# Order of the three products of a split feed-forward: high weights twice in a row, low weights last

## The chip, the core and the metric

The kernel runs on one core of a Trainium2 chip. The metric is the device time of one execution in microseconds (us); where several executions are timed, their median counts. TensorE (PE) multiplies; its weight loads are rows of their own (PEld) in the profile. VectorE (DVE), ScalarE (ACT) and GpSimd (POOL) do the elementwise work, and the queue of SyncE (SP) issues most DMAs.

## The reference

```python
def _attn_ref(q, k, v, w_phi):            # 8 x 8 heads, 576 tokens, head_dim 64
    def phi(x):
        proj = np.einsum('bhsd,df->bhsf', x, w_phi)                # 128 features
        proj = proj - np.max(np.abs(proj), axis=-1, keepdims=True)
        return np.concatenate([np.exp(proj), np.exp(-proj)], axis=-1)
    q_p, k_p = (phi(q), phi(k))
    kv = np.einsum('bhsf,bhsd->bhfd', k_p, v)
    z = np.sum(k_p, axis=2)
    num = np.einsum('bhsf,bhfd->bhsd', q_p, kv)
    den = np.einsum('bhsf,bhf->bhs', q_p, z)[..., None] + 1e-06
    return (num / den).astype(np.float32)

def _moe_ref(x, w_in, w_out, alpha):      # x: 4608 x 512, w_in: 512 x 2048, w_out: 2048 x 512
    h = x @ w_in
    g = np.maximum(h, 0.0) + alpha * np.minimum(h, 0.0)
    return (g @ w_out).astype(np.float32)
```

The attention's output, with its heads laid side by side, is the `x` of the feed-forward. All arrays are float32, and the weights of the feed-forward arrive as 64-bit numbers, which the kernel decodes.

## The kernel before

**Attention.** 32 pairs of heads are worked off one after the other (`attention_units`). Each pair loads its keys and queries, projects them (L302), subtracts the largest magnitude, takes exponentials, sums keys times values (L343) and keys alone (L360, with a tile of ones as the stationary operand), turns the sums and the queries (L375, L386, L389), multiplies (L408, L426), divides, and stores 64 x 2 rows of `x` to HBM.

**Feed-forward.** A number is split into a high part of type fp32r (a rounding copy, `rnd`, L123) and a low part, the rest (a subtraction, `low`, L127). A product of two split matrices is made of three matmuls that add up in one PSUM bank: high by high, and the two mixed ones. Weights of one hidden block `ff` (128 of the 2048 hidden units) are four tiles: `wt[0]` and `wt[1]` are the high and low part of `w_in`, `wt[2]` and `wt[3]` those of `w_out`, and all four are 128 x 512 slots of one SBUF tile. Tokens come in 9 chunks of 512. `gemm1` makes one hidden block of a chunk: four steps over the 512 input features, each of three matmuls with 128 x 128 weights and 512 columns of activations (L498 to L500). ACT then takes two rectifiers out of PSUM (L230, L231), DVE joins them (L235), ACT casts the high part `gh` (L123), and DVE subtracts it to get the low part `gl` (L127). `gemm2` adds one hidden block into one of four output blocks `m`, with three matmuls (L504 to L506).

**Two passes.** The first pass holds the weights of 5 of the 16 hidden blocks in SBUF. Its `gemm1` and `gemm2` triples (names `h`, `o`) for a chunk are strewn between the matmuls of later head pairs, in an order written out by hand: every unit has a due time, and the units are issued by it with the order of PE, SP, DVE and ACT pinned (L733). `x` is cast by ACT and its low part is made by POOL (`split`, `split_low`). The partial sums go to HBM (`part_d`). The second pass, with the other 11 hidden blocks (names `h`, `po`), starts between units of the first (L718 to L723) and has the machine to itself from about 607 us on. There the order within each engine is not pinned: a planner, which simulates the program with costs of its own, sets it, so that one triple's matmuls may stand apart with those of other triples between them. Two hidden blocks lie between a `gemm1` and its `gemm2` (`LAG`), and `gh` and `gl` have three buffers each. At the end of a chunk DVE adds the partial sums to the four banks (L690) and SP stores the result.

**SBUF places in the second pass.** The split `x` of even chunks (`x2hl`) lies in the lower part of each partition, that of odd chunks (`x2h`, `x2l`) in the upper part; `gh`, `gl` and the weights of 8 hidden blocks lie low, those of the last 3 high.

Of the kernel before, what the change touches and what calls it, by code (L numbers as in the profile page):

```python
# [24 lines left out]
NK = DM // P  # L25
# [83 lines left out]
def fused_kernel(ctx: ExitStack, tc: tile.TileContext, kq, v, w_phi, w_in, w_out, alpha, out):  # L109
    nc = tc.nc  # L110
    act, dve, pool, pe = nc.scalar, nc.vector, nc.gpsimd, nc.tensor
# [110 lines left out]
    last = [None]  # L222
# [270 lines left out]
    def gemm1(ps, wt, xs, steps=range(NK)):  # L493
        for n in steps:
            j = NK - 1 - n
            ws = slice(j * P, (j + 1) * P)
            xh, xl = xs[j]
            pe.matmul(ps, lhsT=wt[0][:, ws], rhs=xh, start=n == 0, stop=False)  # L498
            pe.matmul(ps, lhsT=wt[1][:, ws], rhs=xh, start=False, stop=False)  # L499
            pe.matmul(ps, lhsT=wt[0][:, ws], rhs=xl, start=False, stop=n == NK - 1)  # L500

    def gemm2(ps, wt, m, gh, gl, first, last):
        ws = slice(m * P, (m + 1) * P)
        pe.matmul(ps, lhsT=wt[2][:, ws], rhs=gh, start=first, stop=False)  # L504
        pe.matmul(ps, lhsT=wt[3][:, ws], rhs=gh, start=False, stop=False)  # L505
        pe.matmul(ps, lhsT=wt[2][:, ws], rhs=gl, start=False, stop=last)  # L506

    def ffn1_units(c, fg=FG):
        cs = slice(c * C2, (c + 1) * C2)
# [24 lines left out]
        def up(ff, n):  # L534
            if n == 0:
                cur["ps"] = psf.tile([P, C2], F32, tag="f", name=f"h1_{c}_{ff}")
            gemm1(cur["ps"], W[ff], gs[0], (n,))
            if n == NK - 1:
                ga[ff] = act_g(cur["ps"], ff, C2, g1p, g1p, GB, f"1_{c}_{ff}", dve, 3)
                ga[ff][0]()  # L540

        def down(m, ff):
            if ff == 0:
                cur["po", m] = psf.tile([P, C2], F32, tag="f", name=f"o1_{c}_{m}")
            gemm2(cur["po", m], W[ff], m, *gs[ff + 1], ff == 0, ff == NF1 - 1)
# [120 lines left out]
    def up2(c, ff):  # L666
        ps = psf.tile([P, C2], F32, tag="f", name=f"h2_{c}_{ff}")
        gemm1(ps, W[NF1 + ff], xs[c])
        gq[c, ff] = act_g(ps, NF1 + ff, C2, late_pools["x2p"], late_pools["x2r"], G2_BUFS, f"2_{c}_{ff}", dve, 3)
# [6 lines left out]
    def down2(c, ff):  # L676
        cs = slice(c * C2, (c + 1) * C2)
        if ff == 0:
            po[c] = [late_pools["pso"].tile([P, C2], F32, tag=f"o{m}", name=f"po{c}{m}") for m in range(NK)]
        if ff == NF2 - 4:  # L680
            prt[c] = x2b[0].tile([P, NK, C2], F32, tag="pt", name=f"pt{c}")
            ld_ = nc.sync.dma_start(prt[c], part_d[:, :, cs].rearrange("k p s -> p k s"))
            if c > 0:
                tc.keep_in_program_order(ld_)
        gh, gl = gq.pop((c, ff))
        for m in range(NK):
            gemm2(po[c][m], W[NF1 + ff], m, gh, gl, ff == 0, ff == NF2 - 1)
            if ff == NF2 - 1:
                o = prt[c][:, m]
                dve.tensor_tensor(o, po[c][m], o, op=ALU.add)  # L690
                if c == NC2 - 1:
                    nc.sync.dma_start(out[m * P : (m + 1) * P, cs], o)
        if ff == NF2 - 1 and c < NC2 - 1:
            nc.sync.dma_start(out[:, cs].rearrange("(m p) s -> p m s", p=P), prt[c])
# [92 lines left out]
```

## Time and profile before

| | us |
|---|---|
| median of 3 runs (1142.69 to 1146.83) | 1143.23 |
| the profiled execution | 1141.93 |
| its span, first to last instruction | 1139.8 |
| PE busy | 1120.0 (98%) |
| DVE busy | 632.7 (56%) |
| ACT busy | 560.5 (49%) |
| POOL busy | 209.4 (18%) |

The profiled execution lies 2.13 us outside its span, and 1.30 us below the median of the runs. Matmul records overlap, since a matmul's end is modelled; the distance from one start to the next is what a matmul takes on PE. A matmul is two records, a weight load on PEld and the matmul on PE; where the instruction waits for a semaphore, its weight load waits.

### The profile page before, as it was taken

Reading aid. Unit: us, or ns where it says so; the run is one execution under the profiler, and the core shown is the slowest. Engines: PE = TensorE matmul, PEld = TensorE weight load, DVE = VectorE, ACT = ScalarE, POOL = GpSimd, SP = SyncE. Lnnn points to the kernel's source line nnn. Section 1 sums busy time; section 2 is a strip of 40 time slices with the busy share of each in tenths; the row PEclk is TensorE's granted clock in tenths of the full one; section 3 lists DMA queues with packets and bytes.
Section 4 is the critical chain, followed back from the end, with each engine's and each line's share of the span. In section 5 each row is a group of like instructions: output and inputs, shape, how many; then the busy total and the mean of one; then the engine's idle time right before and its main releaser. Section 6 shows DMA issues by size and latency. Waiting matters only on the chain.

```text
span 1139.8 us, 18355 instructions
## 1 busy us (share of the span) xinstructions
PE 1120.0 (98%) x7232; PEld 866.8 (76%) x7232; DVE 632.7 (56%) x978; ACT 560.5 (49%) x1149; POOL 209.4 (18%) x213
## 2 busy tenths in 40 slices
PE   7999999999999999999999999999999999999998
PEld 6766777777777777677778888888888888888886
DVE  7888958798788777835862242424242423333322
ACT  5777655666675765664544332333332323333232
POOL 1345332322324142243540000000000000000000
PEclk9999999999999999999999999999999999999999
DMA  5566264546545364566426030303030302011021
GB/s 190 152 186 213 67 200 154 168 151 209 161 149 190 110 211 152 156 219 207 156 65 221 1 112 1 111 1 111 0 111 1 111 1 87 26 38 74 1 74 37
DMA packets 71605, 130.53 MB, mean 115 GB/s; under 512 B 14432, under 2 KB 22752, under 8 KB 70496
## 3 DMA queue, kind: packets, MB, share of 16 engines
q1 hardware_dynamic: 70080, 120.90, 33.1%
q0 software_dynamic: 1152, 8.39, 2.0%
q8 instruction: 57, 0.93, 0.4%
q14 instruction: 28, 0.23, 0.1%
q10 hardware_dynamic: 288, 0.07, 0.0%
HBM read 92.35 MB, written 36.85 MB: 113 GB/s over the span
## 4 chain that ended last, share of the span: by engine, by line
PE 89%; DVE 5%; DMA 4%; ACT 1%; issue 1%; POOL 0%; SPq 0%; DVEq 0%; ACTq 0%; POOLq 0%
PE h L498 11%; PE h L500 11%; PE h L499 11%; PE po L506 8%; PE po L504 8%; PE po L505 8%; PE kv L343 6%; PE n L408 5%; PE pj L302 5%; PE o L506 3%; PE o L504 3%; PE o L505 3%; PE d L426 3%; PE qt L389 2%; PE kv L360 1%; DVE m L306 1%
## 5 line engine op out<-in xcount | busy, mean ns | idle before, releaser
L235 DVE SCALAR_TENSOR_TENSOR g<-r,aln,g 128x512 f32<-128x512 f32 x144 | 112.5, 781 | 318.5 <-ACT g L231 318.5
L230 ACT ACTIVATE r<-h 128x512 f32<-128x512 f32 x144 | 86.5, 601 | 300.1 <-PE h L500 300.0
L506 PE MATMUL po<-gl,w 128*128 128x512 f32 x396 | 154.6, 392 | 1.5 <-DVE gl L127 1.5
L504 PE MATMUL po<-gh,w 128*128 128x512 f32 x396 | 155.1, 392 | 0.1
L505 PE MATMUL po<-gh,w 128*128 128x512 f32 x396 | 155.0, 391 | 0.0
L127 DVE TENSOR_TENSOR gl<-g,gh 128x512 fp32r<-128x512 f32 x144 | 104.8, 728 | 66.9 <-ACT gh L123 66.5
L123 ACT CAST gh<-g 128x512 fp32r<-128x512 f32 x144 | 90.0, 625 | 84.7 <-DVE g L235 84.6
L506 PEld LDWEIGHTS po<-gl,w 128*128 128x128 f32 x396 | 74.3, 188 | 18.8 <-DVE gl L127 2.4
L504 PEld LDWEIGHTS po<-gh,w 128*128 128x128 f32 x396 | 74.3, 188 | 17.0 <-ACT gh L123 0.5
L231 ACT ACTIVATE g<-h 128x512 f32<-128x512 f32 x144 | 85.9, 596 | 2.6 <-DMA part_d<-os 2.6
L505 PEld LDWEIGHTS po<-gh,w 128*128 128x128 f32 x396 | 74.3, 188 | 16.5
L498 PE MATMUL h<-x2hl,w 128*128 128x512 f32 x220 | 86.0, 391 | 0.0
L500 PE MATMUL h<-x2hl,w 128*128 128x512 f32 x220 | 86.0, 391 | 0.0
L499 PE MATMUL h<-x2hl,w 128*128 128x512 f32 x220 | 85.9, 391 | 0.0
L306 DVE TENSOR_REDUCE m<-pj 128x8 f32<-128x1024 f32 (+1 forms) x66 | 78.2, 1185 | 9.6 <-PE pj L302 9.3
L302 PE MATMUL pj<-w_sb,raw 64*128 64x128 f32 x1024 | 74.5, 286 | 7.5 <-DMA w_sb<-w_phi_dram 4.2
L302 PEld LDWEIGHTS pj<-w_sb,raw 64*128 64x128 f32 x1024 | 65.2, 194 | 21.1 <-issue 14.7
L185 POOL TENSOR_TENSOR aw<-ew,aw 128x256 f32<-128x256 f32 x64 | 56.4, 882 | 128.9 <-DVE ew L180 128.9
L307 DVE TENSOR_TENSOR t<-pj,m 128x1024 f32<-128x1024 f32 (+1 forms) x66 | 78.7, 1192 | 2.3
L504 PE MATMUL o<-gh,w 128*128 128x512 f32 x180 | 76.0, 422 | 2.2 <-ACT os L549 2.0
L498 PE MATMUL h<-xh,w 128*128 128x512 f32 x180 | 75.8, 421 | 0.0
L458 POOL TENSOR_TENSOR s<-s,rr 128x576 f32<-128x576 f32 x32 | 47.5, 1485 | 150.4 <-DMA rr<-rec_d 127.2
(84 smaller groups left out, 2132.3 us busy)
## 6 DMA issues: line engine op xcount, KB each, us to landing
xr<-x_d SPq DMA_DIRECT2D x18, 1024.0 KB
raw<-kq_dram SPq DMA_DIRECT2D x31, 576.0 KB
v<-v_dram SPq DMA_DIRECT2D x32, 320.0 KB
rr<-rec_d SPq DMA_DIRECT2D x64, 144.0 KB
x_d<-s SPq DMA_DIRECT2D x32, 288.0 KB
part_d<-os SPq DMA_DIRECT2D x36, 256.0 KB
pt<-part_d SPq DMA_DIRECT2D x9, 1024.0 KB
raww<-w_in_dram SPq DMA_DIRECT2D x32, 256.0 KB
```

The costliest lines, as they stand in the source:

```text
L123: return act.copy(dst, src)
L127: return eng.tensor_tensor(dst, src, f(hi), op=ALU.subtract)
L230: act.activation(st["r"], ps, AF.Relu, scale=-1.0)
L235: dve.scalar_tensor_tensor(g, st["r"], aln[:, ff : ff + 1], g, op0=ALU.mult, op1=ALU.add)
L302: pe.matmul(dst[h, j], lhsT=c["raw"][hs, ts], rhs=w_sb[hs], start=True, stop=True)
L306: dve.tensor_reduce(m, src, axis=AX.X, op=ALU.max, apply_absolute_value=True)
L498: pe.matmul(ps, lhsT=wt[0][:, ws], rhs=xh, start=n == 0, stop=False)
L499: pe.matmul(ps, lhsT=wt[1][:, ws], rhs=xh, start=False, stop=False)
L500: pe.matmul(ps, lhsT=wt[0][:, ws], rhs=xl, start=False, stop=n == NK - 1)
L504: pe.matmul(ps, lhsT=wt[2][:, ws], rhs=gh, start=first, stop=False)
L505: pe.matmul(ps, lhsT=wt[3][:, ws], rhs=gh, start=False, stop=False)
L506: pe.matmul(ps, lhsT=wt[2][:, ws], rhs=gl, start=False, stop=last)
```

## The change

In both helpers the second and third product change places. What is multiplied and summed is the same, and so are the start and stop flags of the first and last matmul.

```diff
@@ gemm1
             pe.matmul(ps, lhsT=wt[0][:, ws], rhs=xh, start=n == 0, stop=False)
-            pe.matmul(ps, lhsT=wt[1][:, ws], rhs=xh, start=False, stop=False)
-            pe.matmul(ps, lhsT=wt[0][:, ws], rhs=xl, start=False, stop=n == NK - 1)
+            pe.matmul(ps, lhsT=wt[0][:, ws], rhs=xl, start=False, stop=False)
+            pe.matmul(ps, lhsT=wt[1][:, ws], rhs=xh, start=False, stop=n == NK - 1)
@@ gemm2
         pe.matmul(ps, lhsT=wt[2][:, ws], rhs=gh, start=first, stop=False)
-        pe.matmul(ps, lhsT=wt[3][:, ws], rhs=gh, start=False, stop=False)
-        pe.matmul(ps, lhsT=wt[2][:, ws], rhs=gl, start=False, stop=last)
+        pe.matmul(ps, lhsT=wt[2][:, ws], rhs=gl, start=False, stop=False)
+        pe.matmul(ps, lhsT=wt[3][:, ws], rhs=gh, start=False, stop=last)
```

So L499 and L505 of the kernel after multiply the low activations, and L500 and L506 the low weights. In a triple, the first and second matmul now name the same stationary tile.

## Rows read from the trace of the kernel before

**Rows 1.** The page, part 1: engine, busy us, share of the span, instructions
```profile
PE 1120.0 (98%) x7232; PEld 866.8 (76%) x7232; DVE 632.7 (56%) x978; ACT 560.5 (49%) x1149; POOL 209.4 (18%) x213
```

**Rows 2.** Busy time by stretches: us, then each engine's busy us (instructions), PEclk, DMA share, GB/s
```profile
100.00:300.00 200.00, 197.80 (x1674) 144.16 (x1673) 158.68 (x234) 128.68 (x278) 67.12 (x60) 1.00 0.51 160
...
500.00:560.00 60.00, 57.48 (x268) 44.16 (x267) 36.42 (x62) 32.83 (x71) 26.68 (x29) 1.00 0.67 226
...
900.00:1000.00 100.00, 100.00 (x437) 81.83 (x436) 33.43 (x49) 34.65 (x62) 0.00 (x0) 1.00 0.19 64
```

**Rows 3.** Groups by line: names, shapes, count | busy us, mean ns | idle us before, releaser
```profile
L506 PE MATMUL po<-gl,w 128*128 128x512 f32 x396 | 154.6, 392 | 1.5 <-DVE gl L127 1.5
...
L506 PE MATMUL o<-gl,w 128*128 128x512 f32 x180 | 71.7, 398 | 3.5 <-DVE gl L127 3.3
L500 PE MATMUL h<-xl,w 128*128 128x512 f32 x180 | 70.7, 393 | 0.0
...
L505 PEld LDWEIGHTS po<-gh,w 128*128 128x128 f32 x396 | 74.3, 188 | 16.5
...
L360 PEld LDWEIGHTS kv<-z,ones 128*32 128x32 f32 x184 | 3.6, 108 | 3.0 <-issue 0.4
```

**Rows 4.** Waits of PEld: line, releaser, us in total, times, longest us
```profile
PEld o L506 <- DVE gl L127: 7.1, 9, 2.0
...
PEld po L506 <- DVE gl L127: 2.4, 2, 1.8
```

**Rows 5.** Timeline, PEld, 201 to 204 us: start us, us, operation, idle before
```profile
201.78 0.19 PEld L505 LDWEIGHTS o<-gh,w 128*128 128x128 f32 x1
202.01 0.19 PEld L506 LDWEIGHTS o<-gl,w 128*128 128x128 f32 x1
...
202.90 0.19 PEld L505 LDWEIGHTS o<-gh,w 128*128 128x128 f32 x1
203.72 0.19 PEld L506 LDWEIGHTS o<-gl,w 128*128 128x128 f32 x1 [0.62 <-DVE gl L127]
```

**Rows 6.** Timeline, DVE, the same stretch
```profile
201.23 0.68 DVE L127 TENSOR_TENSOR gl<-g,gh 128x512 fp32r<-128x512 f32 x1
...
202.99 0.68 DVE L127 TENSOR_TENSOR gl<-g,gh 128x512 fp32r<-128x512 f32 x1
```

**Rows 7.** Timeline, PEld, two pairs of waits that follow closely
```profile
517.22 0.19 PEld L506 LDWEIGHTS o<-gl,w 128*128 128x128 f32 x1 [0.48 <-DVE gl L127]
...
518.97 0.19 PEld L506 LDWEIGHTS o<-gl,w 128*128 128x128 f32 x1 [1.21 <-DVE gl L127]
...
540.82 0.19 PEld L506 LDWEIGHTS po<-gl,w 128*128 128x128 f32 x1 [1.80 <-DVE gl L127]
...
544.36 0.19 PEld L506 LDWEIGHTS po<-gl,w 128*128 128x128 f32 x1 [0.59 <-DVE gl L127]
```

**Rows 8.** Timeline, DVE and ACT, before the second wait of each pair
```profile
518.24 1.45 DVE L127 TENSOR_TENSOR gl<-g,gh 128x512 fp32r<-128x512 f32 x2
...
542.32 0.60 ACT L231 ACTIVATE g<-h 128x512 f32<-128x512 f32 x1 [2.63 <-DMA part_d<-os]
```

**Rows 9.** Timeline, POOL and PE, a low part of x and its first reader
```profile
548.06 2.76 POOL L127 TENSOR_TENSOR xl<-xr,xh 128x512 fp32r<-128x512 f32 x2
...
551.80 0.39 PE L499 MATMUL h<-xh,w 128*128 128x512 f32 x1
```

**Rows 10.** Timeline, PE, ten matmuls on low x and low weights: first and last
```profile
717.68 0.39 PE L499 MATMUL h<-x2hl,w 128*128 128x512 f32 x1
...
719.72 0.39 PE L499 MATMUL h<-x2hl,w 128*128 128x512 f32 x1
```

**Rows 11.** Timeline, PE, ten matmuls on high x and low weights: first, last
```profile
673.20 0.40 PE L498 MATMUL h<-x2h,w 128*128 128x512 f32 x1
...
675.30 0.39 PE L504 MATMUL po<-gh,w 128*128 128x512 f32 x1
```

## The prediction

> **What bounds the kernel now.** I read the page's first part, then busy time by stretches, then PE's groups by line, then the waits of PE's weight loads, and the timeline around those waits last. The first part gives the bound: PE is busy for 98% of the span, DVE for 56% [rows 1]. The stretches show that it isn't bound in the same way throughout. From 900 to 1000 us, in the second pass, PE has no gap at all at a granted clock of 1.00, the 2.4 GHz level, while DVE and ACT work for a third of the time; around 200 us it is still 99% busy, but DVE is at 79%; between 500 and 560 us PE loses 2.5 of 60 us [rows 2]. So in the second pass only the distance from one matmul to the next counts, and in the first also whether an operand is ready in time. In the second pass 437 records touch those 100 us; two of them only reach in over an edge, so 435 starts lie in it and the mean distance is 100/435 = 229.9 ns.
>
> The reader is to see in the groups that every matmul has its weight load: the page counts 7232 of either [rows 1], and a load takes 188 ns, less than the distance, and lies beside the matmul in front [rows 3]. PE's own idle time names one releaser among the feed-forward's lines that bears on the change: `gl`, ahead of L506, 1.5 us for `po` and 3.3 us for `o` [rows 3]. That is only the visible part. The wait is taken by the weight load, and there it is 7.1 us in 9 times and 2.4 us in 2: eleven waits, 9.5 us [rows 4]. All lie before 545 us or in the rest of the first pass; none is in the second pass proper.
>
> **What the change does, part by part.** *The matmuls.* Per triple, three before and three after, 1152 triples (9 chunks x 16 hidden blocks x 4 steps, once for each helper), no instruction added or gone, the same shapes. PE's stream costs the same if the distance does, taken as 0 here; its two bounds are worked out under the rivals.
>
> *The low activations are needed one matmul sooner.* This is the one cost that the order itself carries. A weight load is issued when the matmul in front of it starts. In a triple today the load for `gl` goes out at the start of the second product; afterwards at the start of the first. Where `gl` is already late, its end doesn't move; behind it there are now two matmuls of the triple left instead of one. So each of the eleven waits grows by one distance, 0.23 us, and pushes everything behind it on PE: the third product, the rest of the triples, and with them ACT, which relieves PSUM. 11 x 0.23 = 2.5 us.
>
> *New waits.* A `gl` that comes ready in the last 0.23 us before its load is late afterwards. Comparing DVE's 144 subtractions with the first load that reads each, I find one: `gl` ends at 201.91 (201.23 + 0.68) [rows 6], its load goes out at 202.01, and in the new order would go out with the load that now starts at 201.78 [rows 5]: a wait of 0.13 us, and up to another 0.1 us because the load isn't hidden any more. I take 0.2 us. The very next one is of the eleven: DVE works until 203.67 [rows 6] and the load starts at 203.72 after 0.62 us [rows 5].
>
> *What comes back.* Two pairs of waits stand so close that the first one's delay runs into the second. At 517.2 and 519.0 us [rows 7] the second wait's DVE work is queued behind DVE work of its own [rows 8]; at 540.8 and 544.4 [rows 7] the second hangs on ACT, which itself waited 2.6 us for a DMA [rows 8]. In both the second wait shrinks by what the first grew: -2 x 0.23 = -0.5 us.
>
> *The other low operand.* `xl` of the first pass is made by POOL far ahead: the tightest of the 36 I find ends at 550.82 (548.06 + 2.76), and its load goes out at 551.80 with the matmul in front [rows 9], 0.98 us later, four distances. The group of its reader shows no idle time [rows 3]. Cost 0. If POOL were a microsecond later there, it would be one wait of the kind above.
>
> *Buffers.* `gh` and `xh` are read until the third product now, so they come free 0.23 us later, `gl` and `xl` sooner. No wait of PE names such a release; the cover is three to five buffers with two hidden blocks between writer and reader. Cost 0; without that cover, 0.23 us per buffer turn. No DMA and no instruction of SP, POOL, ACT or DVE moves in the pinned part.
>
> **Sum.** 2.5 + 0.2 - 0.5 = 2.2 us, between 0 (PE's delay swallowed each time by a later wait on something that PE doesn't feed) and 2.8 (no delay swallowed). On the profiled execution 1141.9 + 2.2 = 1144.1; the median of the runs shown lies 1.3 us above it, so 1143.2 + 2.2 = 1145.4, a change of 0.2%. A difference under 0.5% (5.7 us) is about what a measurement of this kernel can't tell from none, so this forecast is "no change" with a lean to slower.
>
> **Rivals.**
>
> *The second load of the same weights falls away.* Two matmuls in a row now name one stationary tile, so a load could be left out, by the build or in the engine. Price: a matmul without a load can't be shorter than its 512 columns; at one column a cycle of 2.4 GHz, which I assume, that is 213.3 ns, so at most 229.9 - 213.3 = 16.6 ns for each of 1152 second products, 19.1 us; at least 0, since the load of 188 ns is hidden already [rows 3]. At the full price 1145.4 - 19.1 = 1126.3. Against it: all 184 matmuls with the tile of ones as stationary operand, one after another in groups, have 184 loads of their own [rows 3], though at changing places of the array. For it: nothing but the kernel's new order. The Trainium skill ("TensorE: Matmul & The Clock Gate", section "Step-by-step: what each phase is for") says that weights often stay put over many matmuls, and that load and compute are separate so that one can load once and multiply repeatedly. The same page's section "Back-to-back issue gap" gives 518 cycles for an isolated matmul of 512 columns, 215.8 ns; by that, an estimate, the gain would be 16.2 us. By that rule the time falls by over 1%; the trace, with a load for every matmul, does not show it.
>
> *The hand-over gets slower (the case on the other side).* The trace has two distances. Nine distances with `x` in the lower part of SBUF and low weights take 719.72 - 717.68 = 2.04 us, 226.7 ns each [rows 10]; nine with `x` in the upper part and low weights take 2.10 us, 233.3 ns [rows 11]. It seems to depend on which tile streams while which weights are loaded, and the change makes new pairs: high activations beside the load of the same weights again, low ones beside the low weights. Should every pair of the second pass (9 x 11 x 8 x 3 = 2376 matmuls) come out slow, that is 2376 x 3.4 ns = 8.1 us: 1153.5, slower by 0.9%. It decides from about half of them on. Against it: inside either stretch all three kinds of hand-over have the same distance, and the tiles paired anew lie in the same parts of SBUF as before. The mirror image, every pair fast, is 2376 x -3.2 = -7.6 us: 1137.8.
>
> *The planner orders the second pass anew.* Its order is not written down, and a low operand that is due earlier can make it draw triples apart elsewhere. If it then starts each of the 8 later chunks with a wait as long as the longest shown, 2.0 us [rows 4], that is 16 us: 1161. Against it: PE has no gap there, `gl` is made two hidden blocks ahead, and the order has a microsecond and more to give.
>
> *The change doesn't reach the waits*, since all are swallowed: 1143.2. It is inside the forecast's own range.
>
> **Chances and range.** The forecast, waits alone, 0 to 2.8 us: 0.84, own range 1142 to 1148 with the spread of the runs shown, whose highest is 3.6 us over the median. Load left out: 0.04. Slow hand-overs: 0.05; fast ones: 0.03. A worse order: 0.04. Faster by over 0.5% means under 1137.5: load left out, and a little of the fast hand-overs: 0.05. Slower means above 1148.9: slow hand-overs, a worse order at its price, without the part of either that stays small: 0.07. The range of 1141 to 1149 leaves out mainly the outer cases.
>
> **What would show it.** In the changed profile the wait on `gl` should stand at L505 (now the low activations) instead of L506, eleven or twelve times for PEld, each about 0.23 us longer, and the weight loads should still count 7232. L499 and L500 should have no idle time, 900 to 1000 us should hold 436 to 438 matmuls, and the distances in the two shown stretches should be 227 and 233 ns. Fewer loads or over 440 matmuls in those 100 us would make the first rival right; 430 or fewer the second; a gap of PE after 607 us that names `xl`, `x2l` or `gl` the third.

## The result, and the profile after

The kernel after takes 1146.34 us (median of 22 runs, 1143.38 to 1149.01), the kernel before 1143.69 us (22 runs beside them, 1141.42 to 1148.66): a ratio of 1.0019, 95% interval 1.001 to 1.0028, that is 1.1 to 3.2 us slower. Forecast were 2.2 us, called "no change" with a lean to slower.

The first part of the page after, where the counts of matmuls and loads are what they were [rows 1]:

```profile
span 1143.5 us, 18355 instructions
...
PE 1118.3 (98%) x7232; PEld 865.1 (76%) x7232; DVE 636.3 (56%) x978; ACT 560.9 (49%) x1149; POOL 210.6 (18%) x213
```

Groups of the kernel after by line, which answer to [rows 3]. L499 and L505 multiply the low activations now:

```profile
L505 PE MATMUL po<-gl,w 128*128 128x512 f32 x396 | 155.2, 392 | 2.0 <-DVE gl L127 2.0
L506 PE MATMUL po<-gh,w 128*128 128x512 f32 x396 | 154.9, 391 | 0.0
...
L505 PE MATMUL o<-gl,w 128*128 128x512 f32 x180 | 71.6, 398 | 5.5 <-DVE gl L127 5.3
...
L499 PE MATMUL h<-xl,w 128*128 128x512 f32 x180 | 70.5, 392 | 0.0
```

Waits of the weight loads after (line, releaser, us in total, times, longest), beside [rows 4]:

```profile
PEld o L505 <- DVE gl L127: 9.4, 10, 2.2
...
PEld po L505 <- DVE gl L127: 2.7, 2, 2.0
```

The wait on `gl` has gone with its operand from L506 to L505: twelve times and 12.1 us instead of eleven and 9.5. The low part of `x` has still no wait (L499). The second pass shows nothing. Here are its busy time from 900 to 1000 us (columns as in [rows 2]), and the first and tenth of ten matmuls with low and with high `x` [rows 10, 11]:

```profile
900.00:1000.00 100.00, 100.00 (x437) 81.84 (x436) 35.26 (x52) 35.53 (x64) 0.00 (x0) 1.00 0.19 64
```

```profile
720.49 0.39 PE L498 MATMUL h<-x2hl,w 128*128 128x512 f32 x1
...
722.53 0.39 PE L498 MATMUL h<-x2hl,w 128*128 128x512 f32 x1
```

```profile
676.21 0.40 PE L498 MATMUL h<-x2h,w 128*128 128x512 f32 x1
...
678.31 0.40 PE L498 MATMUL h<-x2h,w 128*128 128x512 f32 x1
```

Nine distances are 2.04 and 2.10 us again, 226.7 and 233.3 ns; the count is the same 437.

Two profiles of this kernel can't be subtracted from end to end, since executions differ by microseconds in the first 230 us whatever the kernel. So I read three marks in each profile: A, the start of the same key-value matmul of the attention; B and C, the starts of the first and the last addition of partial sums (L690). First the kernel before (A is the start in the row of the timeline, B and C are the two times in the row of the tile's operations), then the kernel after:

```profile
227.43 1.95 PE L343 MATMUL kv<-xk,v 128*64 128x256 f32 x16
```

```profile
L690 DVE TENSOR_TENSOR pt<-po,pt x36: 681/685/692, 654.0 to 1136.0; 128x512 f32<-128x512 f32 x36
```

```profile
229.24 1.95 PE L343 MATMUL kv<-xk,v 128*64 128x256 f32 x16
```

```profile
L690 DVE TENSOR_TENSOR pt<-po,pt x36: 678/683/692, 657.7 to 1139.7; 128x512 f32<-128x512 f32 x36
```

The same marks of all kernels, us:

| kernel | A | B | C | A to B | B to C |
|---|---|---|---|---|---|
| before | 227.43 | 654.0 | 1136.0 | 426.6 | 482.0 |
| after | 229.24 | 657.7 | 1139.7 | 428.5 | 482.0 |
| e1, gemm1 alone | 230.39 | 656.9 | 1138.9 | 426.5 | 482.0 |
| e2, gemm2 alone | 227.85 | 656.2 | 1138.3 | 428.4 | 482.1 |
| e3, same pairs, low last | 227.78 | 654.7 | 1136.8 | 426.9 | 482.1 |
| e4, low first | 230.63 | 661.4 | 1143.4 | 430.8 | 482.0 |
| e5, held back | 229.40 | 651.1 | 1133.1 | 421.7 | 482.0 |
| e6, places | 229.59 | 655.1 | 1133.8 | 425.5 | 478.7 |
| e7, e5 and e6 | 229.62 | 652.4 | 1131.1 | 422.8 | 478.7 |
| e8, e7 and copy first | 226.28 | 646.2 | 1125.0 | 419.9 | 478.8 |
| e9, copy first | 226.88 | 654.2 | 1136.2 | 427.3 | 482.0 |

The kernel after loses 1.9 us between A and B, where ten of the eleven waits lie, and nothing between B and C, where 2096 of the second pass's 2376 matmuls start. What lies ahead of A, 1.8 us in this pair of profiles, is of the size by which kernels with the very same program up to there differ: e6 reaches A 2.2 us later than the kernel before. A to B isn't free of that either: the five kernels with `gl` third in `gemm2` and no product held back (before, e1, e3, e6, e9) take 425.5 to 427.3 us, and most of their differences arise at one place, near 543 us, where PE hangs on a DMA. So the 1.9 us are also followed from wait to wait, where the prediction is gone through step by step.

### The profile page after: what moved, and what is told of

It reads as the page before. It is cut to its first block, busy times and chain, and to the rows that moved or that the text cites. A ratio compares the mean times of both kernels' runs of the same rounds, so it can differ in the third digit from the quotient of the medians.

```text
span 1143.5 us, 18355 instructions
## 1 busy us (share of the span) xinstructions
PE 1118.3 (98%) x7232; PEld 865.1 (76%) x7232; DVE 636.3 (56%) x978; ACT 560.9 (49%) x1149; POOL 210.6 (18%) x213
## 3 DMA queue, kind: packets, MB, share of 16 engines
q0 software_dynamic: 1152, 8.39, 2.0%
## 4 chain that ended last, share of the span: by engine, by line
PE 88%; DVE 5%; DMA 4%; ACT 1%; issue 1%; POOL 0%; SPq 0%; DVEq 0%; ACTq 0%; POOLq 0%
PE h L498 11%; PE h L499 11%; PE h L500 11%; PE po L505 8%; PE po L506 8%; PE po L504 8%; PE kv L343 6%; PE n L408 5%; PE pj L302 5%; PE o L505 3%; PE o L504 3%; PE o L506 3%; PE d L426 2%; PE qt L389 2%; DVE m L306 1%; PE kv L360 1%
## 5 line engine op out<-in xcount | busy, mean ns | idle before, releaser
L505 PE MATMUL po<-gl,w 128*128 128x512 f32 x396 | 155.2, 392 | 2.0 <-DVE gl L127 2.0
L506 PE MATMUL po<-gh,w 128*128 128x512 f32 x396 | 154.9, 391 | 0.0
L505 PEld LDWEIGHTS po<-gl,w 128*128 128x128 f32 x396 | 74.3, 188 | 19.2 <-DVE gl L127 2.7
L506 PEld LDWEIGHTS po<-gh,w 128*128 128x128 f32 x396 | 74.3, 188 | 16.4
L500 PE MATMUL h<-x2hl,w 128*128 128x512 f32 x220 | 86.0, 391 | 0.0
L499 PE MATMUL h<-x2hl,w 128*128 128x512 f32 x220 | 85.9, 391 | 0.0
L505 PE MATMUL o<-gl,w 128*128 128x512 f32 x180 | 71.6, 398 | 5.5 <-DVE gl L127 5.3
```

The costliest lines, as they stand in the source:

```text
L499: pe.matmul(ps, lhsT=wt[0][:, ws], rhs=xl, start=False, stop=False)
L500: pe.matmul(ps, lhsT=wt[1][:, ws], rhs=xh, start=False, stop=n == NK - 1)
L505: pe.matmul(ps, lhsT=wt[2][:, ws], rhs=gl, start=False, stop=False)
L506: pe.matmul(ps, lhsT=wt[3][:, ws], rhs=gh, start=False, stop=last)
```

## The experiments

The theory is that the cost comes from the eleven waits alone, because `gl` is needed one matmul sooner. The rival is a cost of the hand-over: the same weights loaded twice in a row, with a little lost (or a load saved) at each of 1152 triples.

**e1_up_only.** The new order in `gemm1` only:

```diff
 pe.matmul(ps, lhsT=wt[0][:, ws], rhs=xh, start=n == 0, stop=False)
-pe.matmul(ps, lhsT=wt[1][:, ws], rhs=xh, start=False, stop=False)
-pe.matmul(ps, lhsT=wt[0][:, ws], rhs=xl, start=False, stop=n == NK - 1)
+pe.matmul(ps, lhsT=wt[0][:, ws], rhs=xl, start=False, stop=False)
+pe.matmul(ps, lhsT=wt[1][:, ws], rhs=xh, start=False, stop=n == NK - 1)
```

> The new order in gemm1 alone; gemm2 keeps the old one. Theory of the waits (the whole cost comes from gl being needed one matmul sooner): 0 us against the kernel before, within 1 us either way, since xl has 0.98 us and more in hand; waits on gl stay at L506, eleven, about 9.5 us for the weight loads. Rival of the hand-over (a cost spread evenly over the 1152 triples, since the same weights are loaded twice in a row): half of what the whole change costs, 1.3 us, and the distances of matmuls in the second pass longer than 227 and 233 ns.

Measured: 1144.12 us, ratio 1.0004 (0.9992 to 1.0016). From A to B 426.5 us against 426.6, B to C 482.0 against 482.0. Half of the triples in the new order cost nothing that shows in the profile; the interval of the timing, -0.9 to 1.8 us, would by itself still hold the rival's 1.3 us.

**e2_down_only.** The same exchange in `gemm2` only:

```diff
 pe.matmul(ps, lhsT=wt[2][:, ws], rhs=gh, start=first, stop=False)
-pe.matmul(ps, lhsT=wt[3][:, ws], rhs=gh, start=False, stop=False)
-pe.matmul(ps, lhsT=wt[2][:, ws], rhs=gl, start=False, stop=last)
+pe.matmul(ps, lhsT=wt[2][:, ws], rhs=gl, start=False, stop=False)
+pe.matmul(ps, lhsT=wt[3][:, ws], rhs=gh, start=False, stop=last)
```

> The new order in gemm2 alone; gemm1 keeps the old one. Theory of the waits: the whole cost, 2.2 us (1.5 to 3.2) over the kernel before; the weight loads at L505 wait for gl eleven or twelve times, about 12 us, nothing changes after 607 us. Rival of the hand-over: half of it, 1.3 us, part of it in the second pass.

Measured: 1146.65 us, ratio 1.0025 (1.001 to 1.0039): the whole cost. Between A and B 428.4 us, 1.8 more than before; nothing in the second pass. Its loads wait eleven times, 11.2 us in all:

```profile
PEld o L505 <- DVE gl L127: 8.5, 9, 2.2
...
PEld po L505 <- DVE gl L127: 2.7, 2, 2.0
```

**e3_low_last_pairs.** Low weights first in both helpers, so that the two products with high weights stand together as in the change, but the low activations come third as before:

```diff
-pe.matmul(ps, lhsT=wt[2][:, ws], rhs=gh, start=first, stop=False)
-pe.matmul(ps, lhsT=wt[3][:, ws], rhs=gh, start=False, stop=False)
+pe.matmul(ps, lhsT=wt[3][:, ws], rhs=gh, start=first, stop=False)
+pe.matmul(ps, lhsT=wt[2][:, ws], rhs=gh, start=False, stop=False)
 pe.matmul(ps, lhsT=wt[2][:, ws], rhs=gl, start=False, stop=last)
```

> Both helpers with low weights first, then high weights with high and then low activations: the same weights twice in a row as in the change, but the low activations third as in the kernel before. Theory of the waits: 0 us against the kernel before (within 1 us), eleven waits on gl of about 9.5 us at L506. Rival of the hand-over: the full 2.7 us of the change. Rival of the load that falls away: fewer than 7232 weight loads, up to 19 us faster.

Measured: 1143.21 us, ratio 0.9991 (0.9978 to 1.0005). The first part of its page and its waits:

```profile
PE 1120.4 (98%) x7232; PEld 866.7 (76%) x7232; DVE 633.2 (56%) x978; ACT 560.9 (49%) x1149; POOL 212.4 (19%) x213
```

```profile
PEld o L506 <- DVE gl L127: 7.4, 10, 2.0
...
PEld po L506 <- DVE gl L127: 2.4, 2, 1.8
```

The reader is to see three things: no load falls away with the same weights twice in a row, the waits have their old size (9.8 us), and the time is that of the kernel before: the interval ends 0.6 us above it, and the rival asked for 2.7 us. So the pairing is neither the cost nor a gain; what costs is where the low activations stand. That decides between the two theories. Every matmul brings its own load here, 7232 of either, and the same weights twice in a row 1152 times saved nothing. The Trainium skill ("TensorE: Matmul & The Clock Gate", section "Step-by-step: what each phase is for") says that load and compute are separate so that one can load once and multiply repeatedly; in this program's trace that did not happen.

**e4_low_first.** The dose doubled: in `gemm2` the low activations first of the three, then the two with `gh`.

> gemm2 with the product of the low activations first of the three, then the two of the high ones; gemm1 as before. The dose is doubled: gl is needed two matmuls sooner than in the kernel before. Theory of the waits: each of the eleven waits 0.46 us longer, 5.1 us, plus about 0.4 us for the one gl that just missed, less about 0.9 us where two waits follow closely: 4.5 us (3 to 6), all before 607 us. Rival of the hand-over (the same weights twice in a row, as in the change): no more than the change, 2.7 us or, for gemm2 alone, 1.3 us.

Measured: 1148.53 us, ratio 1.0035 (1.002 to 1.005), slower by 2.3 to 5.7 us. Between A and B 430.8 us, 4.2 more than before where the change itself has 1.9; nothing in the second pass. One distance earlier costs 1.9, two cost 4.2.

**e5_hold_back.** The other way round, from the kernel before. In the first pass `gl`'s product of a triple is kept back by two triples; for the first three blocks of the second pass it comes behind the high products of all four banks:

```diff
+            gemm2_high(cur["po", m], W[ff], m, gs[ff + 1][0], ff == 0)
+            held.append((m, ff))
+            if ff == NF1 - 1:
+                own = [h for h in held if h[0] == m]
+                for h in own:
+                    held.remove(h)
+                    low_part(*h, h is own[-1])
+            elif len(held) > HOLD:
+                low_part(*held.pop(0), False)
...
+        if c == 0 and ff < NB:
+            for m in range(NK):
+                gemm2_high(po[c][m], W[NF1 + ff], m, gh, ff == 0)
+            for m in range(NK):
+                pe.matmul(po[c][m], lhsT=W[NF1 + ff][2][:, m * P : (m + 1) * P], rhs=gl, start=False, stop=False)
+            return
```

> From the kernel before, the other way round: in the first pass the product of the low activations of a gemm2 triple is held back and issued two triples later (at the latest with the last triple of its output bank); for the first three hidden blocks of the second pass it comes after the high products of all four banks. So gl is needed about 1.4 to 2 us later. Theory of the waits: of the eleven waits (9.5 us for the weight loads) at most the longest, 2.0 us, leaves a rest of about 0.6 us; 8 us goes, some of it comes back as other waits of PE on work that it now reaches sooner: 3 to 7 us faster than the kernel before. If PE's waits for gl were only cover for other lateness: less than 1 us.

Measured: 1139.06 us, ratio 0.9957 (0.9943 to 0.997), 3.4 to 6.5 us faster. Waits of its loads, among which those on `gl` are nearly gone; a few on ACT have taken a part of their place, as PE now gets there sooner:

```profile
PEld o L511 <- ACT gh L124: 2.0, 3, 0.9
...
PEld po L511 <- ACT gh L124: 1.4, 1, 1.4
...
PEld h L499 <- ACT os L569: 1.2, 1, 1.2
...
PEld po L710 <- DVE gl L128: 0.4, 1, 0.4
...
PEld o L552 <- DVE gl L128: 0.2, 1, 0.2
```

**e6_places.** To see what the two distances hang on: the kernel before with its order, the split `x` of odd chunks in the lower part of SBUF, `gh` and `gl` of the last three hidden blocks in the upper part.

```diff
-                    xhp = x2b[0].tile([P, 2, C2], F32R, tag="xh", name=f"x2h{c}{j}")
-                    xlp = x2b[0].tile([P, 2, C2], F32R, tag="xl", name=f"x2l{c}{j}")
+                    xhp = late_pools["x2h"].tile([P, 2, C2], F32R, tag="xh", name=f"x2h{c}{j}")
+                    xlp = late_pools["x2h"].tile([P, 2, C2], F32R, tag="xl", name=f"x2l{c}{j}")
...
+        gp = late_pools["x2p" if ff < NA + ND else "x2q"]
...
+    late_pools["x2h"] = ctx.enter_context(tc.tile_pool(name="x2h", bufs=2))
+    late_pools["x2q"] = ctx.enter_context(tc.tile_pool(name="x2q", bufs=2, side="right"))
```

> The kernel before with its order, but other places in SBUF in the second pass: the split x of odd chunks in the lower part of the partition, beside the weights of 8 of the 11 hidden blocks, and gh and gl of the other 3 blocks in the upper part, beside their weights. If the distance of two matmuls is 233 ns where the tile that streams and the weights loaded meanwhile lie in different halves, and 227 where they lie in the same: 375 such pairs are left of 890, so 515 x 6.7 ns = 3.4 us faster, all after 620 us, with the stretch of the high x at 227 ns. If place has nothing to do with it: 0 us and the distances as before.

Measured: 1140.01 us, ratio 0.9962 (0.9949 to 0.9976). B to C is 3.3 us shorter. Ten matmuls with the `x` that was high, first and tenth, and 900 to 1000 us:

```profile
673.29 0.39 PE L498 MATMUL h<-x2h,w 128*128 128x512 f32 x1
...
675.33 0.39 PE L498 MATMUL h<-x2h,w 128*128 128x512 f32 x1
```

```profile
900.00:1000.00 100.00, 100.00 (x440) 82.31 (x439) 32.94 (x48) 35.06 (x63) 0.00 (x0) 1.00 0.18 64
```

The stretch that took 233.3 ns a matmul takes 226.7, and 440 matmuls fit where 437 did.

**e7_hold_and_places.** Both.

> The held-back products of the first pass and the places of the second together. They touch different stretches, so the gains should add: 6 to 10 us faster than the kernel before.

Measured: 1134.78 us, ratio 0.9912 (0.9896 to 0.9929), 8.1 to 11.9 us faster: they add.

**e9_copy_first and e8_hold_places_copy.** All profiles so far share one more wait of PE, at about 150 us. ACT first casts the next chunk's `x`, which waits for a DMA, and only then copies a finished bank out, for which PE waits. PEld in the kernel before:

```profile
151.14 0.19 PEld L504 LDWEIGHTS o<-gh,w 128*128 128x128 f32 x1 [2.45 <-ACT os L549]
```

One number lets the copy go first; e9 does it on the kernel before, e8 on e7:

```diff
-FX = (0.95, 0.75, 0.55, 0.35)
+FX = (0.84, 0.75, 0.55, 0.35)
```

> The later first cast alone, on the kernel before. If the wait of PE on the copy at 150 us sets 2 us of the time and, with the clock that falls after it in some executions, part of the spread between executions (1141.1 to 1148.6 us in 33 runs): 2 us faster than the kernel before (1 to 4), and a spread smaller than its 7 us. The waits on gl stay, eleven, about 9.5 us. If not: 0 us.

Measured: 1141.12 us, ratio 0.9984 (0.9975 to 0.9992), 0.9 to 2.9 us faster. PEld at that place in e9:

```profile
150.33 0.19 PEld L504 LDWEIGHTS o<-gh,w 128*128 128x128 f32 x1 [0.47 <-ACT os L549]
```

The wait is 0.47 us instead of 2.45, and the gain is of its size. That the spread would shrink isn't shown: 4.5 us in its 11 runs, 2.6 us in the 15 of the kernel before beside them.

> The held-back products and the places, and ACT's first cast of a chunk's x due 0.11 of a head pair later (0.84 before the chunk instead of 0.95), so that in the first chunk ACT copies the finished banks out before it queues behind the cast that waits for the DMA of x. In the runs so far PE stood 2.0 to 2.6 us at about 150 us for that copy, and where it stood 2.3 us or longer the granted clock was 0.55 to 0.76 in the next 2.5 us, which cost another 1.6 us. If that wait is what it seems: 2 to 4 us faster than the two changes together, a wait on the copy at 150 us under 0.5 us, the granted clock 1.00 there. If PE then waits for something else that the DMA feeds: no gain.

Measured: 1130.55 us, ratio 0.9902 (0.9885 to 0.9919), 9.3 to 13.1 us faster than the kernel before; the wait on the copy is gone and the clock there is 1.00:

```profile
152.00:154.50 2.50, 2.50 (x40) 1.88 (x41) 1.34 (x6) 2.50 (x5) 1.48 (x2) 1.00 0.75 252
```

Its median is the lowest of all, and it beats both kernels of the study. That it is 2 to 4 us faster than e7, as expected, isn't shown: against their own runs of the kernel before, e7 has 0.9912 and e8 0.9902, and the intervals overlap.

## Why the prediction was right, step by step

**PE's distance unchanged, 0.** Right: B to C is 482.0 us before and after, the 7232 matmuls write their tiles in the same order in both traces, and e3, with the same pairing and no loss, shows it without the waits. The rivals of a load that falls away and of a slower hand-over are out; so is the planner's new order as a cost. The prediction's mean distance came from a count that was off by one: 436 matmuls start between 900 and 1000 us, not 435, 229.3 ns apart. The rivals' prices shift by up to 1.4 us with it, and nothing else rests on it.

**Eleven waits, one distance each, 2.5 us.** Right in place, number and size. Followed through both profiles, nine of the ten waits behind A each set PE back by another 0.16 to 0.25 us, and one by nothing (the second of the first pair below); the eleventh wait lies ahead of A, beside the `gl` that just missed (below). The doubled dose gives 4.2 us and holding back turns the sign.

**What comes back, 0.5 us.** Right in e2, half right in the kernel after. The pair at 517 and 519 us did as said. The load's waits after:

```profile
519.86 0.19 PEld L505 LDWEIGHTS o<-gl,w 128*128 128x128 f32 x1 [0.70 <-DVE gl L127]
521.61 0.19 PEld L505 LDWEIGHTS o<-gl,w 128*128 128x128 f32 x1 [1.22 <-DVE gl L127]
```

The first has grown from 0.48 to 0.70, the second is 1.22 after 1.21 [rows 7]; two distances of cost became one. At the pair at 541 and 544 us there is one more wait between the two, on `gh`, which ACT makes. First that wait in the kernel before, then the three waits in the kernel after, then the last two of them in e2:

```profile
543.47 0.19 PEld L504 LDWEIGHTS po<-gh,w 128*128 128x128 f32 x1 [0.52 <-ACT gh L123]
```

```profile
543.61 0.19 PEld L505 LDWEIGHTS po<-gl,w 128*128 128x128 f32 x1 [2.02 <-DVE gl L127]
546.52 0.19 PEld L504 LDWEIGHTS po<-gh,w 128*128 128x128 f32 x1 [0.54 <-ACT gh L123]
547.41 0.19 PEld L505 LDWEIGHTS po<-gl,w 128*128 128x128 f32 x1 [0.70 <-DVE gl L127]
```

```profile
545.05 0.19 PEld L504 LDWEIGHTS po<-gh,w 128*128 128x128 f32 x1 [0.28 <-ACT gh L123]
545.94 0.19 PEld L505 LDWEIGHTS po<-gl,w 128*128 128x128 f32 x1 [0.70 <-DVE gl L127]
```

In e2 the wait on `gh` is 0.24 us shorter and gives the first wait's distance back, as the prediction said. In the kernel after it is as long as before, nothing comes back, and PE's lag grows by 0.23 at each of the two. ACT waits there for the DMA that stores `os` [rows 8], and that DMA's end moves against PE from one execution to the next: over this place e3 and e9, with `gl` third as before, lose 0.7 and 0.8 us against the kernel before, and e6 gains 0.7. I had taken the DMA as something that PE doesn't feed; it stores a copy of a PSUM bank that PE has filled, so it may move with PE. Which of the two holds isn't shown. With both pairs, the sum for the ten waits behind A is 10 x 0.23 - 0.5 = 1.8, with one pair 2.1; measured are 1.8 in e2 and 1.9 in the kernel after.

**The `gl` that just missed, 0.2 us.** It is late, but the term should have been 0: the wait behind it swallows it. In the kernel after, the load that just missed and the next of the eleven wait

```profile
204.03 0.19 PEld L505 LDWEIGHTS o<-gl,w 128*128 128x128 f32 x1 [1.36 <-DVE gl L127]
...
205.29 0.19 PEld L505 LDWEIGHTS o<-gl,w 128*128 128x128 f32 x1 [0.17 <-DVE gl L127]
```

and the second `gl` of DVE, for which the second load waits, is

```profile
204.56 0.68 DVE L127 TENSOR_TENSOR gl<-g,gh 128x512 fp32r<-128x512 f32 x1
```

The second load starts when this `gl` is ready, whatever the first wait took; its own wait has shrunk from 0.62 us [rows 5] to 0.17. The prediction named this neighbour and did not count it as a third pair.

Over the two waits PE's lag behind the kernel before grows by 0.88 us, from 0.93 to 1.81. One distance, 0.23, is that of the wait that was there before. The rest is DVE's: its second `gl` ends at 205.24 us instead of 203.67 [rows 6], 1.57 later, when PE was only 0.93 late. The loss begins a few operations ahead on DVE, where the add L329 took 0.85 us longer than in the kernel before. This add, then GpSimd's multiply that runs beside it; after:

```profile
196.69 2.43 DVE L329 TENSOR_TENSOR y<-xk 128x1024 f32<-128x1024 f32 x1
```

```profile
196.64 1.41 POOL L458 TENSOR_TENSOR s<-s,rr 128x576 f32<-128x576 f32 x1 [4.75 <-DMA raw<-kq_dram]
```

and in e2:

```profile
196.21 1.26 DVE L329 TENSOR_TENSOR y<-xk 128x1024 f32<-128x1024 f32 x1
```

In the kernel before, this add took 1.58 us. In e2 DVE's second `gl` ends 0.21 us later than there and PE comes 0.45 us later; DVE is 0.24 us ahead by that, which cancels the distance, and PE loses nothing over the two waits. With `gl` third as before the same place moves PE by -0.3 us (e6) to 0.4 (e1, e3). So what happens here beyond the one distance is the execution's and not the change's; in the kernel after it hangs on when a DMA let POOL go.

**`xl` and buffers, 0.** Right: e1.

Of the three terms, then, 2.5 held, 0.2 was nothing, and 0.5 was between 0.2 and 0.5: 2.0 to 2.3 us. That 2.2 was met so closely is in part luck, as the small terms are smaller than what single executions do at their places, and the interval of the timing, 1.1 to 3.2 us, can't tell them apart.

What the prediction did not weigh is how far executions differ at these places and ahead of the change's first instruction. It didn't touch the sign: the prediction held that less than 0.5% can't be told from none, but with 22 runs of each kernel the interval, 1.001 to 1.0028, leaves out a ratio of 1.

## What to carry to other kernels

In a chain of matmuls into one bank, put the operand that is made last into the last product: here every place that it moved forward cost about one matmul distance at nearly every wait that was already there, and nothing where it was early. Before asking what a reordering does to the engine that is busy, count the waits on the operands that it moves, in the row of the weight loads and not only in that of the matmuls; here they said 9.5 us where the matmuls' row said 4.8. And a wait can be moved away as cheaply as it was moved in: holding the low product back (e5) was worth about twice what the change cost.

## What the runs showed of the hardware that was not expected

**Places in SBUF set the distance of matmuls.** With the tile that streams in one part of the partition and the weights that are loaded meanwhile in the other, a matmul of 512 columns takes 233.3 ns; in the same part, 226.7. e6 moved tiles, and the stretch changed from one to the other. (The last three blocks got buffers of their own by it, but PE has no gap there in either kernel.) Sorted by these two places, as the program sets them, the kernel before has 803 distances between B and C with the two apart, 233.5 ns in the mean, and 1292 with the two together, 227.6; in e6 they are 332 with 233.6 and 1763 with 227.3. 471 such pairs removed at 6.67 ns are 3.1 us; B to C shows 3.3.

**Two elementwise engines in each other's way.** DVE's add of two SBUF operands takes 1.22 us alone and 2.43 with GpSimd's multiply beside it, which takes 1.41 us. The one that begins second pays. In the eleven traces the multiply began first beside 31 of these adds: it took 1.41 or 1.42 us each time, and in all but the shortest overlaps the add lost the whole time side by side but 0.13 us. Beside 54 adds it began second: the add took 1.22 us each time, and the multiply up to 2.45 us. The Trainium skill ("Advanced Engine Details and Errata", section "GPSIMD Details") says that Pool shares a read and a write interface with DVE, and that instructions with two SBUF inputs conflict; the trace agrees, and its number is that DVE got almost nothing done meanwhile where it came second.

**A stall can cost the clock as well, and its length alone doesn't tell.** At 150 us PE stands idle for the copy. In the kernel before it stood for 2.0 us and the granted clock stayed at 1.00, the 2.4 GHz level. In e1 it stood for 2.6 us, and afterwards matmuls started 0.43 us apart instead of 0.23: the clock of the next 2.5 us is 0.58, most of it at the 1.2 GHz level. Timeline of e1, and its busy time with PEclk as the third number from the end:

```profile
152.19 0.62 PE L504 MATMUL o<-gh,w 128*128 128x512 f32 x1 [2.58 <-ACT os L549]
152.60 0.63 PE L505 MATMUL o<-gh,w 128*128 128x512 f32 x1
153.03 0.63 PE L506 MATMUL o<-gl,w 128*128 128x512 f32 x1
```

```profile
149.00:152.00 3.00, 0.61 (x3) 0.17 (x1) 0.00 (x0) 0.97 (x2) 0.00 (x0) 1.00 0.80 179
152.00:154.50 2.50, 2.31 (x6) 1.83 (x7) 0.22 (x1) 2.50 (x6) 2.34 (x2) 0.58 0.54 168
```

e4, e5 and e7 show the same (0.55, 0.69 and 0.76 in that stretch), the kernels before and after, e2, e3 and e6 don't. The expectation of e8 put the fall at stalls of 2.3 us and longer, and the stalls at 2.0 to 2.6 us; by PE's rows they are 1.7 (e2, e3) to 2.6. Here is the matmul behind the stall in the kernel after, then in e4:

```profile
152.08 0.50 PE L504 MATMUL o<-gh,w 128*128 128x512 f32 x1 [2.15 <-ACT os L549]
```

```profile
152.41 0.79 PE L504 MATMUL o<-gl,w 128*128 128x512 f32 x1 [2.16 <-ACT os L549]
```

After 2.15 us the clock stayed at 1.00, after 2.16 it was 0.55. What decides, and whether it is this that makes the spread between executions, was not shown.
